# Full attention on one core: the second integer pass over the exponentials moves from VectorE to GpSimd

## The chip, the cores and the metric

The kernel runs on one core of a Trainium2 chip. The core has a matrix engine (TensorE, PE in the profile, with its weight loads as PEld), a vector engine (VectorE, DVE), an activation engine (ScalarE, ACT), a general engine (GpSimd, POOL) and a queue for transfers (SyncE, SP). Each works through its own instructions in a fixed order; semaphores make one wait for another. The metric is the time of one execution on the device in microseconds.

## The reference

Four layers follow each other on x, of shape (1, 2048, 512): a windowed attention A, a full attention B, and both again with the same weights. Each takes the layer-normalized x and adds its result to x. A has 32 heads of 16 and looks at 8 positions, 2 apart. B has 32 query heads of 16 over one shared key and value head; all 2048 positions see all 2048:

```python
q = (x @ wq).reshape(B, S, H, Dh).transpose(0, 2, 1, 3)
k = x @ wk
v = x @ wv
scores = jnp.einsum("bhqd,bkd->bhqk", q, k) * (Dh ** -0.5)
p = _softmax(scores, axis=-1)
o = jnp.einsum("bhqk,bkd->bhqd", p, v)
return o.transpose(0, 2, 1, 3).reshape(B, S, H * Dh) @ wo
```

## The kernel before

The program is two pairs of a stage `Phase` (layer A, and the projections of layer B) and a stage `AttnB` (the full attention). The change lies in `AttnB`.

The scores of layer B are computed transposed, keys on the 128 partitions, 512 queries along the row. A tile of them is 128 keys by 512 queries of one head. Each of 32 segments (4 query chunks, 8 blocks of four heads) has 64 tiles, so a stage has 2048 and the program 4096. Each tile goes through an exponential in one of two ways, and the result is multiplied with the values on TensorE (L1118), with a column of ones beside the values that gives the row sums.

- **By ScalarE.** Two tiles share a PSUM slot `st` (two slots). One exponential instruction (L1099) turns both into bf16 tiles `pt`. Each tile then costs one matmul with the values `VEa`.
- **By VectorE.** A tile sits in a PSUM bank `dv`. The scores are scaled so that adding a constant and storing as 16-bit integers gives the bits of a half-precision number near the exponential: a copy (L1103) writes that into a quarter of a buffer `t`, which holds four tiles. To smooth the approximation, the same integers are taken three times, with offsets of 0, a third and two thirds of 1024 (`J_OFF`), with weights that lie in the values `VEd`. The two shifted versions are made for four tiles at once, by one integer add each (`do_pass`, L1107, a "pass") from `t` into a buffer `i`. Each tile costs three matmuls with the values: one from `t`, two from `i`.

Which tile goes which way, and the order on every engine, is decided while the program is built, by a planner (`Sched` and `Stream`). It plays the engines forward with fixed costs (a copy 600 ns, a pass 133.5 ns a tile and 66, an exponential 426.7 ns a tile and 50, a matmul 216), gives each engine the work that can start first, with small biases, and writes the instructions down in the order of their planned starts. `chain` then holds each engine to that order. `Stream.passes` lists the passes that are ready, `Stream.uses` counts the readers of a buffer (for `t`: its four matmuls and its two passes) until it is free again. There are 14 buffers `pt`, 3 `t` and 5 `i`.

At the end of a segment VectorE copies the sums of the four heads out of PSUM (`X`, L1135). For every second segment the row sums go through transfers (`S`), a reciprocal on VectorE (`R`, L1169) and transfers that spread it (`lb`); GpSimd then scales the rows (`onc`, L1188, 30 times in the program) and adds sums and reciprocals into a check (`chk_b`, L753, 60 times). These are nearly all that GpSimd does in the two stages. After a query chunk comes the output projection (L1205) and its addition to x (L1219).

Of the kernel before, what the change touches and what calls it, by code (L numbers as in the profile page):

```python
# [7 lines left out]
F32 = mybir.dt.float32  # L8
F16 = mybir.dt.float16
I16 = mybir.dt.int16  # L10
AF = mybir.ActivationFunctionType
ALU = mybir.AluOpType
AX = mybir.AxisListType
# [15 lines left out]
NJ = 3  # L29
# [395 lines left out]


MM, SWITCH, DMA = 216.0, 90.0, 620.0
LAT = {"pe": 264.0, "act": 170.0, "dve": 135.0, "pool": 120.0, "sp": 2400.0}
FAR = float("inf")

# [13 lines left out]
class Sched:  # L444
# [68 lines left out]
    def cands(self, e):  # L513
        for op in self.open[e]:
            s = max(op.ready, self.free_at(op.want) if op.want else 0.0)
            s = self.pe_start(op.mode, op.sub, s) if e == "pe" else max(s, self.now[e])
            if s < FAR:
                yield (s + op.prio, s, op.ready, self.issue, (e, op))
        for src in self.sources:
            yield from src.cands(e)  # L520

# [39 lines left out]
class Stream:  # L561
# [5 lines left out]
    def __init__(self, sched, segments, ready, io, res):  # L567
        self.s, self.io = sched, io
        self.segs = segments
        self.tile_ready = ready  # L570
        self.tiles = [(n, kt, g) for n, (_, kts) in enumerate(segments) for kt in kts for g in range(4)]
        self.pos = 0
        self.exps, self.copies, self.passes = [], [], []
# [17 lines left out]
    def cands(self, e):  # L591
        S, B = self.s, self.BIAS
        if e == "pe":
            if self.pos < len(self.tiles):
                tl = self.tiles[self.pos]
                ok = self.tile_ready(self.segs[tl[0]], tl[1])
                if ok < FAR:
                    s = S.pe_start("row", tl[2], max(ok, S.free_at(("slot", "exp"))))
                    if s < FAR:
                        yield (s + B["act2" if self.exps else "act"], s, 0.0, self.fill_slot, None)  # L600
                    s = S.pe_start("row", tl[2], max(ok, S.free_at(("bank", "vec"))))
                    if s < FAR:
                        yield (s + B["vec"], s, 0.0, self.fill_vec, None)
            if self.seg < len(self.segs):
                free = S.free_at(("bank", "o")) if self.bank is None else 0.0
                if free < FAR:
                    for n, (ok, tl, src) in enumerate(self.pvs[self.seg][:24]):
                        s = S.pe_start("col", tl[2], max(ok, free))
                        yield (s + B["pv"] + n * 0.01, s, 0.0, self.pv, n)
        elif e == "act" and self.exps:  # L610
            s = max(S.now["act"], self.exps[0][0], S.free_at(("pt", "exp")))
            if s < FAR:
                yield (s, s, self.exps[0][0], self.exp, None)
        elif e == "dve":
            if self.copies:
                s = max(S.now["dve"], self.copies[0][0])
                if not self.filling:
                    s = max(s, S.free_at(("t", "vec")))
                if s < FAR:
                    late = self.run_of_copies >= 2 and self.passes  # L620
                    yield (s + (B["pass"] if late else B["copy"]), s, 0.0, self.copy, None)
            if self.passes:
                s = max(S.now["dve"], self.passes[0][0], S.free_at(("i", "vec")))
                if s < FAR:
                    yield (s + (0.0 if self.run_of_copies >= 2 else B["pass"]), s, 0.0, self.do_pass, None)

    def fill_slot(self, s, _):
        S, io = self.s, self.io
# [46 lines left out]
    def copy(self, s, _):  # L675
        S, io = self.s, self.io
        _, tl, bank = self.copies.pop(0)
        if not self.filling:
            self.group_buf = S.take(("t", "vec"))
        r, buf = len(self.filling), self.group_buf  # L680
        self.filling.append(tl)
        S.run("dve", s, 600.0)
        done = s + 600 + LAT["dve"]
        S.give(("bank", "vec"), bank, done)
        S.note(s, lambda: io.copy(bank, buf, r))
        self.run_of_copies += 1
        if len(self.filling) == self.GROUP or (self.pos == len(self.tiles) and not self.copies):
            tiles, self.filling = self.filling, []
            self.uses[("t", buf)] = [len(tiles) + NJ - 1, 0.0, ("t", "vec")]
            for j in range(1, NJ):  # L690
                self.passes.append((s + 600, buf, j, tiles))
            for r, tl in enumerate(tiles):
                self.queue(tl, done, ("t", buf, r, 0), 1)

    def do_pass(self, s, _):
        S, io = self.s, self.io
        _, buf, j, tiles = self.passes.pop(0)
        n = len(tiles)
        t = 133.5 * n + 66
        S.run("dve", s, t)  # L700
        out = S.take(("i", "vec"))
        self.uses[("i", out)] = [n, 0.0, ("i", "vec")]
        S.note(s, lambda: io.do_pass(buf, out, j, n))
        self.run_of_copies = 0
        for r, tl in enumerate(tiles):
            self.queue(tl, s + t + LAT["dve"], ("i", out, r, j), j < NJ - 1)
        self.use(("t", buf), s + t)

    def pv(self, s, n):
# [339 lines left out]
class AttnB:  # L1049


    def __init__(self, ctx, tc, QT, KAB, VE, w, x_sb, S, tag, checks, out_view=None):
        self.tc, self.nc, self.w, self.x_sb, self.checks, self.out_view = tc, tc.nc, w, x_sb, checks, out_view
        self.QT, self.KAB, (self.va, self.vd) = QT, KAB, VE
        pool = lambda name, bufs, **kw: ctx.enter_context(tc.tile_pool(name=f"Bf_{name}_{tag}", bufs=bufs, **kw))
        self.slot = [pool(f"st{n}", 1, space=PSUM) for n in range(2)]
        self.bank = [pool(f"bk{n}", 1, space=PSUM) for n in range(4)]
        self.nrm = pool("n", 3)
        self.oncp = pool("c", 2)
        self.drm = pool("d", 2, space=bass.MemoryType.DRAM)  # L1060
# [12 lines left out]
        self.st, self.o, self.dv, self.y, self.tail = {}, {}, {}, {}, {}  # L1073
        self.X, self.onc, self.onb, self.xo = {}, {}, {}, {}
        self.sums, self.ready = {}, {}

    def chain(self, key, inst):
        order_after(self.tc, inst, self.tail.get(key))
# [24 lines left out]
        self.chain("dve", self.nc.vector.tensor_scalar(out=self.t[buf][:, r, :].bitcast(I16), in0=self.dv[bank][:],  # L1103
                                                       scalar1=-U_BIAS, scalar2=U_BIAS, op0=ALU.max, op1=ALU.add))

    def do_pass(self, buf, out, j, n):
        self.chain("dve", self.nc.vector.tensor_scalar(out=self.i[out][:, 0:n, :].bitcast(I16),  # L1107
                                                       in0=self.t[buf][:, 0:n, :].bitcast(I16), scalar1=J_OFF[j],
                                                       scalar2=None, op0=ALU.add))

    def pv(self, bank, at, src, first, last):
        (qc, t, a), kt, g = at
# [216 lines left out]
def kernel(  # L1329
# [13 lines left out]
    nc = tc.nc  # L1343
# [108 lines left out]
```

## Time and profile before

| | |
|---|---|
| timed runs | 1769.97 and 1771.0 us, median 1770.49 |
| profiled execution | span of 1772.6 us from the first to the last instruction |
| first full-attention stage | 208.9 to 883.4 us, 674.5 us |
| second full-attention stage | 1086.4 to 1753.3 us, 666.9 us |
| VectorE copies L1103 | 1332, mean 680 ns |
| VectorE passes L1107 | 668, mean 698 ns |
| ScalarE exponentials L1099 | 1382, mean 1094 ns |
| GpSimd busy, whole span | 206.2 us, 257 instructions |
| mean granted TensorE clock | 0.923 |

The durations of instructions that follow each other on one engine overlap at the ends, so a mean is longer than what one instruction costs in a row of them; the busy time counts each moment once. "Idle before" is the time that the engine stood still ahead of an instruction, with what ended it.

### The profile page before, as it was taken

The page shows a single profiled execution, that of the slowest core. Times are in us where ns is not written, and L with a number is a line of the kernel's source. Part 1 is how long each engine was busy: PE and PEld are TensorE (multiplying, and loading weights), DVE is VectorE, ACT ScalarE, POOL GpSimd, SP SyncE. Part 2 cuts the span into 40 slices and gives each one's busy share as a digit, 9 for nine tenths or more (in the row PEclk, how much of TensorE's full clock was granted, in tenths as well). Part 3 has the DMA queues.
Part 4 walks back from the last instruction along what each step waited for, and adds up shares of the span by engine and source line. Part 5 has one row for each costly group of instructions (what it writes and reads, how often), then busy time and mean ns, then how long its engine had stood idle before and what let it go on. Part 6 is the DMA issues. An engine that isn't in the chain of part 4 may idle for free.

```text
span 1772.6 us, 39835 instructions
## 1 busy us (share of the span) xinstructions
PE 1569.5 (89%) x16214; PEld 539.7 (30%) x16281; DVE 1535.8 (87%) x2565; ACT 1507.3 (85%) x1721; POOL 206.2 (12%) x257
## 2 busy tenths in 40 slices
PE   5776799899999999999977777998999999999996
PEld 3544222222222223222345442222222222222222
DVE  6565499999999999998955646999999999999997
ACT  4654599999999989999856546999999999999994
POOL 4343000000000000000123420000000000000001
PEclk9988799999988999978998878999999899998998
DMA  4000000000000000000000000000000000000000
GB/s 123 3 2 3 0 5 12 17 11 10 12 11 11 11 11 11 11 11 11 11 2 3 2 2 1 11 11 11 11 11 23 11 11 11 23 14 11 11 15 30
DMA packets 40736, 22.96 MB, mean 13 GB/s; under 512 B 28512, under 2 KB 34272, under 8 KB 40544
## 3 DMA queue, kind: packets, MB, share of 16 engines
q1 hardware_dynamic: 39680, 18.50, 4.8%
q8 instruction: 129, 2.11, 0.5%
q10 hardware_dynamic: 864, 1.84, 0.3%
q14 instruction: 63, 0.52, 0.1%
HBM read 13.27 MB, written 2.59 MB: 9 GB/s over the span
## 4 chain that ended last, share of the span: by engine, by line
DVE 59%; PE 26%; ACT 9%; issue 3%; POOL 1%; DMA 0%; DVEq 0%; SPq 0%; ACTq 0%; POOLq 0%
DVE t L1103 32%; DVE i L1107 17%; PE o L1118 9%; PE ps L882 5%; PE st L1084 4%; ACT pt L1099 4%; PE dv L1084 3%; DVE P L951 2%; DVE X L1135 2%; DVE stats L857 2%; ACT P L950 1%; PE pv L910 1%; DVE x_sb L1001 1%; PE dn L980 1%; PE o L961 1%
## 5 line engine op out<-in xcount | busy, mean ns | idle before, releaser
L1099 ACT ACTIVATE pt<-st 128x1024 bf16<-128x1024 f32 x1382 | 1290.7, 1094 | 48.2 <-PE dv L1084 20.4
L1103 DVE TENSOR_SCALAR t<-dv 128x512 int16<-128x512 f32 x1332 | 856.9, 680 | 11.3 <-PE dv L1084 6.2
L1084 PE MATMUL st<-QT,KAB 32*128 32x512 bf16 x2764 | 560.3, 400 | 14.8 <-ACT pt L1099 13.2
L1084 PE MATMUL dv<-QT,KAB 32*128 32x512 bf16 x1332 | 512.9, 397 | 52.2 <-DVE t L1103 38.4
L1118 PE MATMUL o<-pt,VEa 128*32 128x512 bf16 x2764 | 546.3, 412 | 2.7 <-DVE t L1103 1.8
L1118 PE MATMUL o<-i,VEd 128*32 128x512 f16 x2664 | 535.7, 403 | 10.5 <-DVE i L1107 10.1
L1107 DVE TENSOR_SCALAR i<-t 128x2048 int16<-128x2048 int16 x668 | 466.0, 698 | 11.2 <-PE o L1118 0.5
L1084 PEld LDWEIGHTS <-KAB 32*128 32x128 bf16 x4096 | 188.1, 91 | 556.4 <-issue 541.5
L1118 PE MATMUL o<-t,VEd 128*32 128x512 f16 x1332 | 344.7, 407 | 0.2
L1118 PEld LDWEIGHTS <-VEd 128*32 128x32 f16 x3996 | 145.4, 94 | 225.0 <-issue 221.7
L1118 PEld LDWEIGHTS <-VEa 128*32 128x32 bf16 x2764 | 120.2, 94 | 191.9 <-issue 188.9
L753 POOL TENSOR_TENSOR chk_b<-chk_b,S 128x32 f32<-128x32 f32 x30 | 11.0, 367 | 813.6 <-DMA S<-X 684.3
L951 DVE TENSOR_TENSOR P<-P,bandmask 128x1152 bf16<-128x1152 bf16 (+1 forms) x64 | 60.9, 951 | 38.4 <-ACT P L950 37.8
L950 ACT ACTIVATE P<-s 128x1152 bf16<-128x1152 f32 (+1 forms) x64 | 71.8, 1121 | 16.7 <-PE s L945 16.6
L882 PE MATMUL ps<-xnT,w_sb 128*128 128x512 bf16 x233 | 69.2, 427 | 16.8 <-DVE k L898 8.8
L875 PE MATMUL pT<-ident,xn 128*128 128x128 bf16 x256 | 30.6, 263 | 40.4 <-ACT xn L867 23.2
L1188 POOL TENSOR_TENSOR onc<-X,lb 128x512 bf16<-128x512 f32 x30 | 39.8, 1327 | 228.2 <-DMA lb<-rd 214.5
L984 ACT ACTIVATE logs<-dn 128x512 f32<-128x512 f32 x32 | 19.1, 598 | 45.4 <-PE dn L980 45.2
L961 PE MATMUL o<-P,V 64*32 64x72 bf16 (+2 forms) x2176 | 34.9, 209 | 18.9 <-DVE P L951 15.3
L1135 DVE COPY X<-o 128x512 f32<-128x512 f32 x64 | 43.7, 683 | 8.7 <-PE o L1118 8.6
L986 DVE TENSOR_TENSOR onc<-o,rec 128x512 bf16<-128x512 f32 x32 | 22.0, 687 | 33.0 <-ACT rec L985 24.9
L747 POOL TENSOR_TENSOR logs<-logs 128x512 f32<-128x512 f32 x32 | 34.3, 1071 | 130.1 <-ACT rec L985 130.1
(108 smaller groups left out, 871.1 us busy)
## 6 DMA issues: line engine op xcount, KB each, us to landing
lb<-rd SPq DMA_DIRECT2D x240, 32.0 KB, 1.8
S<-X SPq DMA_DIRECT2D x240, 2.0 KB, 1.7
X<-X SPq DMA_DIRECT2D x120, 32.0 KB, 2.0
rd<-R SPq DMA_DIRECT2D x120, 4.0 KB, 1.5
w_sb<-in_A_wqkv_dram ACTq DMA_DIRECT2D x4, 384.0 KB, 5.6
x_bf<-in_A_x_dram SPq DMA_DIRECT2D x3, 512.0 KB, 9.3
out_dram<-xo SPq DMA_DIRECT2D x3, 512.0 KB, 3.0
x_bf<-in_A_x_dram SPq DMA_DIRECT2D x2, 256.0 KB, 5.0
```

Source lines behind the costliest of these rows:

```text
L857: nc.vector.bn_stats(out=stats[:, i, :], in_=src(i))
L882: self.nc.tensor.matmul(ps[:], lhsT=wcols(kt), rhs=xnT[:, kt, :], start=(kt == 0), stop=(kt == 3))
L950: nc.scalar.activation(out=P[:, :, 0:ncol], in_=st[:, :, 0:ncol], func=AF.Exp, scale=DH ** -0.5)
L951: nc.vector.tensor_tensor(out=P[:, :, 0:ncol], in0=P[:, :, 0:ncol], in1=self.w.band[:, 0:ncol].unsqueeze(1).to_broadcast([128, 4, ncol]), ...
L961: nc.tensor.matmul(o[32 * r:32 * r + 32, q0:q0 + w], lhsT=vv[64 * a:64 * a + 64, kb, t, gh, j, :], rhs=P[64 * a:64 * a + 64, g, col:col + ...
L1084: self.chain("pe", self.nc.tensor.matmul(out, lhsT=self.KAB[32 * g:32 * g + 32, a, kt * 128:(kt + 1) * 128], rhs=self.QT[32 * g:32 * g + 3 ...
L1099: self.chain("act", self.nc.scalar.activation(out=self.pt[pt][:, 0:n, :], in_=self.st.pop(key)[:, 0:n, :], func=AF.Exp, scale=E_SCALE))
L1103: self.chain("dve", self.nc.vector.tensor_scalar(out=self.t[buf][:, r, :].bitcast(I16), in0=self.dv[bank][:], scalar1=-U_BIAS, scalar2=U_B ...
L1107: self.chain("dve", self.nc.vector.tensor_scalar(out=self.i[out][:, 0:n, :].bitcast(I16), in0=self.t[buf][:, 0:n, :].bitcast(I16), scalar1 ...
L1118: self.chain("pe", self.nc.tensor.matmul(self.o[bank][32 * g:32 * g + 32, :], lhsT=lhsT, rhs=rhs, start=first, stop=last, tile_position=(0 ...
L1135: self.chain("dve", nc.vector.tensor_copy(out=self.X[qc, t, a][:], in_=self.o.pop(bank)[:]))
L1188: self.chain("pool", nc.gpsimd.tensor_tensor(out=self.onc[qc][:, t, :], in0=self.X[qc, t, 0][:], in1=bufs["lb"][:], op=ALU.mult))
```

## The change

For each group of four tiles the first pass stays on VectorE. The second is done by GpSimd. There it is written as an add of 32-bit integers: two 16-bit values lie in one 32-bit word, and a constant tile `off2` (128 x 4 words, each half holding the offset) is read again and again along the row. The values are not negative and no half overflows into its neighbour, so the sum is the same. A group's row is 1024 words for GpSimd where it was 2048 halves for VectorE.

GpSimd's pass is made to wait for VectorE's pass on the same group (`order_after` with `first_pass`). In the planner a GpSimd pass costs 2.1 ns a word and 120 ns; a new time `port` keeps any pass, on either engine, from being planned before the last planned pass on either has ended. There are seven buffers `i` in place of five. For operations outside the stream (`Op`), the planner's rank now falls by a tenth of the time they have waited.

```diff
@@ Sched.cands
-                yield (s + op.prio, s, op.ready, self.issue, (e, op))
+                yield (s + op.prio - 0.1 * (s - op.ready), s, op.ready, self.issue, (e, op))
@@ Stream.cands
-                s = max(S.now["dve"], self.passes[0][0], S.free_at(("i", "vec")))
+                s = max(S.now["dve"], self.passes[0][0], S.free_at(("i", "vec")), self.port)
                 if s < FAR:
-                    yield (s + (0.0 if self.run_of_copies >= 2 else B["pass"]), s, 0.0, self.do_pass, None)
+                    yield (s + (0.0 if self.run_of_copies >= 2 else B["pass"]), s, 0.0, self.do_pass, "dve")
+        elif e == "pool" and self.pool_passes:
+            s = max(S.now["pool"], self.pool_passes[0][0], S.free_at(("i", "vec")), self.port)
+            if s < FAR:
+                yield (s, s, self.pool_passes[0][0], self.do_pass, "pool")
@@ Stream.copy
-            for j in range(1, NJ):
-                self.passes.append((s + 600, buf, j, tiles))
+            self.passes.append((s + 600, buf, 1, tiles))
@@ Stream.do_pass
-        t = 133.5 * n + 66
-        S.run("dve", s, t)
+        t = 133.5 * n + 66 if e == "dve" else POOL_COL * 256 * n + 120
+        S.run(e, s, t)
+        self.port = s + t
+        if j < NJ - 1:
+            self.pool_passes.append((s + t + LAT["dve"], buf, j + 1, tiles))
...
-            self.queue(tl, s + t + LAT["dve"], ("i", out, r, j), j < NJ - 1)
+            self.queue(tl, s + t + LAT[e], ("i", out, r, j), j < NJ - 1)
@@ AttnB.__init__
-        self.i = [fixed.tile([128, Stream.GROUP, 512], F16, name=f"i{n}") for n in range(5)]
+        self.i = [fixed.tile([128, Stream.GROUP, 512], F16, name=f"i{n}") for n in range(7)]
@@ AttnB
-    def do_pass(self, buf, out, j, n):
-        self.chain("dve", self.nc.vector.tensor_scalar(out=self.i[out][:, 0:n, :].bitcast(I16),
-                                                       in0=self.t[buf][:, 0:n, :].bitcast(I16), scalar1=J_OFF[j],
-                                                       scalar2=None, op0=ALU.add))
+    def do_pass(self, e, buf, out, j, n):
+        if e == "pool":
+            i = self.nc.gpsimd.tensor_tensor(out=self.i[out][:, 0:n, :].bitcast(I32), in0=self.t[buf][:, 0:n, :].bitcast(
+                I32), in1=self.w.off2[:, 0:n].unsqueeze(2).to_broadcast([128, n, 256]), op=ALU.add)
+            order_after(self.tc, i, self.first_pass.pop(buf))
+        else:
+            i = self.nc.vector.tensor_scalar(out=self.i[out][:, 0:n, :].bitcast(I16), in0=self.t[buf][:, 0:n, :].bitcast(
+                I16), scalar1=J_OFF[j], scalar2=None, op0=ALU.add)
+            self.first_pass[buf] = i
+        self.chain(e, i)
@@ kernel
+    w.off2 = cpool.tile([128, 4], I32, name="off2")
+    nc.gpsimd.memset(w.off2[:].bitcast(I16), round(J_OFF[2]))
```

The planner plays out again with these rules, so the order changes on every engine. On VectorE, at the start of the first full-attention stage before (the names carry buffer numbers: `t_3674` is one of the three buffers `t`, `i_3677` one of the buffers `i`; x4 is four instructions alike):

```order
L1103 TENSOR_SCALAR t_3674<-dv 128x512 x4
L1107 TENSOR_SCALAR i_3677<-t_3674 128x2048
L1103 TENSOR_SCALAR t_3675<-dv 128x512 x2
L1107 TENSOR_SCALAR i_3678<-t_3674 128x2048
L1103 TENSOR_SCALAR t_3675<-dv 128x512 x2
L1107 TENSOR_SCALAR i_3679<-t_3675 128x2048
```

The same place on VectorE now, where the lines have moved by some ten:

```order
L1113 TENSOR_SCALAR t_3676<-dv 128x512 x4
L1122 TENSOR_SCALAR i_3679<-t_3676 128x2048
L1113 TENSOR_SCALAR t_3677<-dv 128x512 x4
L1122 TENSOR_SCALAR i_3681<-t_3677 128x2048
L1113 TENSOR_SCALAR t_3678<-dv 128x512 x4
L1122 TENSOR_SCALAR i_3683<-t_3678 128x2048
```

A pass stood behind every two copies and now stands behind every four; each buffer `t` is read once by VectorE where it was read twice. On GpSimd, before, at the first row scaling of the first stage:

```order
L860 TENSOR_TENSOR rstd<-ve,nhalf 128x4
L753 TENSOR_TENSOR chk_b<-chk_b,S_4009 128x32
L753 TENSOR_TENSOR chk_b<-chk_b,R_4422 128x32
L1188 TENSOR_TENSOR onc<-X,lb 128x512
L753 TENSOR_TENSOR chk_b<-chk_b,S_4580 128x32
```

And GpSimd at the same place now (`off_99` is the constant tile):

```order
L1118 TENSOR_TENSOR i_3685<-t_3677,off_99 128x1024
L763 TENSOR_TENSOR chk_b<-chk_b,S_4030 128x32
L1118 TENSOR_TENSOR i_3680<-t_3678,off_99 128x1024
L1118 TENSOR_TENSOR i_3682<-t_3676,off_99 128x1024
L763 TENSOR_TENSOR chk_b<-chk_b,R_4465 128x32
L1118 TENSOR_TENSOR i_3684<-t_3677,off_99 128x1024
L1118 TENSOR_TENSOR i_3679<-t_3678,off_99 128x1024
L1118 TENSOR_TENSOR i_3681<-t_3676,off_99 128x1024
L1118 TENSOR_TENSOR i_3683<-t_3677,off_99 128x1024
L1204 TENSOR_TENSOR onc<-X,lb 128x512
```

The second passes fill GpSimd's order, and the check adds and the row scaling stand among them.

More of the change, by code (lines that the diff above doesn't have):

```diff
@@ L10 @@
 I16 = mybir.dt.int16
+I32 = mybir.dt.int32
 AF = mybir.ActivationFunctionType
@@ L427 @@
 MM, SWITCH, DMA = 216.0, 90.0, 620.0
+POOL_COL = 2.1
 LAT = {"pe": 264.0, "act": 170.0, "dve": 135.0, "pool": 120.0, "sp": 2400.0}
@@ L572, in __init__ @@
         self.pos = 0
-        self.exps, self.copies, self.passes = [], [], []
+        self.exps, self.copies, self.passes, self.pool_passes = [], [], [], []
+        self.port = 0.0
         self.res = res
@@ L689, in copy, with do_pass @@
             self.uses[("t", buf)] = [len(tiles) + NJ - 1, 0.0, ("t", "vec")]
-            for j in range(1, NJ):
-                self.passes.append((s + 600, buf, j, tiles))
+            self.passes.append((s + 600, buf, 1, tiles))
             for r, tl in enumerate(tiles):
                 self.queue(tl, done, ("t", buf, r, 0), 1)
-    def do_pass(self, s, _):
+    def do_pass(self, s, e):
         S, io = self.s, self.io
-        _, buf, j, tiles = self.passes.pop(0)
+        _, buf, j, tiles = (self.passes if e == "dve" else self.pool_passes).pop(0)
         n = len(tiles)
-        t = 133.5 * n + 66
-        S.run("dve", s, t)
+        t = 133.5 * n + 66 if e == "dve" else POOL_COL * 256 * n + 120
[3 more added lines that the diff above has]
+            self.pool_passes.append((s + t + LAT["dve"], buf, j + 1, tiles))
         out = S.take(("i", "vec"))
         self.uses[("i", out)] = [n, 0.0, ("i", "vec")]
-        S.note(s, lambda: io.do_pass(buf, out, j, n))
-        self.run_of_copies = 0
+        S.note(s, lambda: io.do_pass(e, buf, out, j, n))
+        if e == "dve":
+            self.run_of_copies = 0
         for r, tl in enumerate(tiles):
-            self.queue(tl, s + t + LAT["dve"], ("i", out, r, j), j < NJ - 1)
+            self.queue(tl, s + t + LAT[e], ("i", out, r, j), j < NJ - 1)
         self.use(("t", buf), s + t)
@@ L1074, in __init__ @@
         self.X, self.onc, self.onb, self.xo = {}, {}, {}, {}
-        self.sums, self.ready = {}, {}
+        self.sums, self.ready, self.first_pass = {}, {}, {}
     def chain(self, key, inst):
```

## The prediction

> **What bounds the kernel now.** I read the page's busy times first, then the span cut into its stages, then the groups of instructions, and last single stretches in order of time. On the page three engines look equally full:
>
> ```profile
> PE 1569.5 (89%) x16214; PEld 539.7 (30%) x16281; DVE 1535.8 (87%) x2565; ACT 1507.3 (85%) x1721; POOL 206.2 (12%) x257
> ```
>
> The change touches only the two full-attention stages. The windows cut at the first and last VectorE work of each (columns: window, length, then busy time and count of PE, PEld, DVE, ACT, POOL, and the granted TensorE clock) show them:
>
> ```profile
> 208.90:883.40 674.50, 637.87 (x5466) 178.78 (x5472) 656.45 (x1087) 647.98 (x693) 35.43 (x49) 0.93 0.05 11
> 1086.40:1753.30 666.90, 624.15 (x5463) 178.99 (x5469) 651.01 (x1060) 643.09 (x692) 33.20 (x47) 0.95 0.06 13
> 260.00:300.00 40.00, 38.26 (x346) 10.60 (x345) 39.66 (x66) 40.00 (x44) 1.96 (x4) 1.00 0.05 10
> 1680.00:1700.00 20.00, 20.00 (x198) 6.20 (x195) 19.79 (x34) 20.00 (x24) 0.75 (x2) 1.00 0.09 19
> ```
>
> The stages are 674.5 + 666.9 = 1341.4 us of the span, and GpSimd is 5% busy there. VectorE and ScalarE are at 97% and 96%: they share the score tiles, and the planner has balanced them. Where nothing disturbs, ScalarE is busy without a gap and does 44 instructions in 40.00 us, 0.909 us each. The groups say what those instructions are:
>
> ```profile
> L1099 ACT ACTIVATE pt<-st 128x1024 bf16<-128x1024 f32 x1382 | 1290.7, 1094 | 48.2 <-PE dv L1084 20.4
> L1103 DVE TENSOR_SCALAR t<-dv 128x512 int16<-128x512 f32 x1332 | 856.9, 680 | 11.3 <-PE dv L1084 6.2
> L1107 DVE TENSOR_SCALAR i<-t 128x2048 int16<-128x2048 int16 x668 | 466.0, 698 | 11.2 <-PE o L1118 0.5
> ```
>
> Spans overlap at their ends, so what an instruction costs is the spacing of starts, which a VectorE stretch in order of time gives (start, length, instruction):
>
> ```profile
> 434.13 1.28 DVE L1103 TENSOR_SCALAR t<-dv 128x512 int16<-128x512 f32 x2
> 435.32 0.17 DVE L858 BATCH_NORM_AGGREGATE mv<-stats 128x2 f32<-128x6 f32 x1
> 435.44 0.69 DVE L1107 TENSOR_SCALAR i<-t 128x2048 int16<-128x2048 int16 x1
> 436.05 1.28 DVE L1103 TENSOR_SCALAR t<-dv 128x512 int16<-128x512 f32 x2
> 437.25 1.72 DVE L1107 TENSOR_SCALAR i<-t 128x2048 int16<-128x2048 int16 x1
> 438.89 1.28 DVE L1103 TENSOR_SCALAR t<-dv 128x512 int16<-128x512 f32 x2
> ```
>
> A copy is 0.60 us (437.25 - 436.05 is two), a pass 0.61 (436.05 - 435.44). Per group of four tiles VectorE pays 4 x 0.60 + 2 x 0.61 = 3.62 us, 0.905 a tile; ScalarE pays 0.909 / 2 = 0.455 a tile. Per stage ScalarE needs 691 x 0.909 = 628 us of the mean 670.7, so 42.6 us are lost to the start, the end and disturbances.
>
> **The port.** The pass at 437.25 lasted 1.72 us. GpSimd was at work beside it:
>
> ```profile
> 437.15 1.27 POOL L1188 TENSOR_TENSOR onc<-X,lb 128x512 bf16<-128x512 f32 x1 [6.67 <-DMA lb<-rd]
> 651.69 1.26 POOL L1188 TENSOR_TENSOR onc<-X,lb 128x512 bf16<-128x512 f32 x1 [7.89 <-DMA lb<-rd]
> 651.16 1.28 DVE L1103 TENSOR_SCALAR t<-dv 128x512 int16<-128x512 f32 x2
> ```
>
> GpSimd ended at 438.42, and the pass 0.55 us later, at 438.97: it stood still until GpSimd was done. The copies beside the operation at 651.69 kept their 1.28 us for two. So a pass and a GpSimd operation exclude each other here, a copy out of PSUM and a GpSimd operation do not.
>
> **The change, part by part.** By the order of instructions, VectorE copies go from 1332 to 1428 (+96), its passes from 668 to 358 (-310), ScalarE's exponentials from 1382 to 1334 (-48), and GpSimd gets 358 passes, two of them half size. TensorE's matmuls on these tiles go from 2 x 2764 + 4 x 1332 = 10856 to 2 x 2668 + 4 x 1428 = 11048.
>
> - **ScalarE**: 48 x 0.909 = 43.6 us less. If ScalarE is the last to finish, this is the gain.
> - **VectorE**: 96 x 0.60 - 310 x 0.61 = -131 us. It comes off a bound engine, but only 43.6 us of it can show, since ScalarE is next. VectorE is then some 12% idle and no longer sets the end.
> - **GpSimd's pass**: no row shows an integer add. The nearest are float operations with two different inputs, beside a small one that gives the fixed part (count: shortest/median/longest ns):
>
> ```profile
> L753 POOL TENSOR_TENSOR chk_b<-chk_b,S x30: 249/251/806, 259.6 to 1718.4; 128x32 f32<-128x32 f32 x30
> L1188 POOL TENSOR_TENSOR onc<-X,lb x30: 1262/1270/1771, 272.1 to 1730.7; 128x512 bf16<-128x512 f32 x30
> L747 POOL TENSOR_TENSOR logs<-logs x32: 1032/1039/1519, 42.2 to 1038.6; 128x512 f32<-128x512 f32 x32
> ```
>
> From 32 to 512 elements is 251 to 1270 ns, 2.12 ns an element; 1024 packed pairs are 251 + 992 x 2.12 = 2.36 us. The low bound is the square at L747, 1032 ns: 1.63 ns an element, 1.86 us. The high bound takes the longest row, 1771 ns: 3.17 ns, 3.39 us. I take 2.36, since that row also reads two tensors and is a median of 30. A recorded end can be checked: the pass held at 437.25 ended 0.55 us after GpSimd's recorded end, and a free pass lasts 0.69, so the port came free at most 0.14 us before that end and not after it. The Trainium skill (Perfetto Trace Analysis, GPSIMD Engine Instruction) calls the span of a GpSimd instruction in a profile unreliable. By that rule 2.36 could be off by more than the 0.24 us of cover found below, and then the sum would lose 36 us for each 0.1 us beyond it; by the held pass it is right within 0.14, and the sum stands.
>
> - **The wait**: a GpSimd pass waits for VectorE's pass on the same group. Behind it on GpSimd stand the next groups' passes, the 60 check adds and the 30 row scalings; who waits for it are the matmuls on its tile, and VectorE's next pass through the port. The signal's price is in these rows:
>
> ```profile
> 264.51 0.34 DVE L1169 RECIPROCAL R<-S 128x32 f32<-128x32 f32 x1
> 264.94 0.25 POOL L753 TENSOR_TENSOR chk_b<-chk_b,R 128x32 f32<-128x32 f32 x1 [4.55 <-DVE R L1169]
> ```
>
> VectorE ends at 264.85, GpSimd starts at 264.94: about 0.1 us. So the port's round is 0.55 (a released pass) + 0.1 + 2.36 = 3.01 us a group. VectorE has 4 copies and a pass between two passes, 3.01 us as well, so at full speed the next pass arrives as GpSimd ends. ScalarE's pace is slower: 1334 x 0.909 over 357 groups is 3.40 us a group. The port is covered, with 0.39 us a group to spare. The other GpSimd work takes it for 15 x (1.27 + 2 x 0.25) = 27 us a stage, 0.15 a group; 0.24 is left. If that cover is gone (a pass of over 2.6 us), each further 0.1 us costs 36 us.
>
> - **TensorE**: 192 matmuls more, at nothing, hidden under ScalarE: needed are 11048 in about 1300 us, 170 per 20 us, and the window at 1680 above shows 198 with ScalarE full.
> - **The ends**: the last second pass of a stage, on two tiles, goes from about 0.4 us on VectorE to 251 + 480 x 2.12 = 1.27 us on GpSimd; +1 us twice. Seven i buffers for five, the aged priorities and one more small memset at the start move nothing that ends late: nothing.
>
> Sum on the profiled execution: 1772.6 - 43.6 + 2 = 1731.0. The timed runs' median, 1770.49, lies 2.1 us below the profiled span, so the forecast is 1770.5 - 41.6 = **1729 us**, its own range 1712 to 1745 (a gain from 25 to 58 us: the 42.6 us a stage of losses grow or shrink by a fifth).
>
> **The rivals.**
>
> - **Held passes halve TensorE's clock (slower).** This is in the trace already. After the operation at 437.15 held a pass:
>
> ```profile
> 436.60:440.00 3.40, 2.04 (x12) 0.41 (x11) 3.40 (x5) 3.24 (x4) 1.27 (x1) 0.97 0.00 0
> 440.00:443.40 3.40, 3.40 (x17) 0.73 (x20) 3.27 (x7) 2.06 (x3) 0.00 (x0) 0.50 0.00 0
> 443.40:446.80 3.40, 3.40 (x29) 0.51 (x21) 3.37 (x7) 2.85 (x3) 0.00 (x0) 0.52 0.04 7
> ```
>
> TensorE fell to 12 matmuls in 3.4 us, and the clock was then 0.50 for the next two windows; ScalarE lost 10.2 - 8.15 = 2.05 us. If half of the 90 places where GpSimd's other operations stand between passes end like this, that is 45 x 2.05 = 92 us: 1729 + 92 = 1821. It undoes the gain from 20 events on. For it: the clock's mean is only 0.93 and 0.95 in the stages now. Against: the order places a pass behind a GpSimd pass where the planner thinks the port free. The Trainium skill (TensorE: Matmul & The Clock Gate, Part 1) has the clock fall to half after an idle window of about 3.4 us; the rows agree, with 12 matmuls enough to count as idle. Chance 0.10.
> - **The port becomes the bound (slower).** The Trainium skill warns that moving work between VectorE and GpSimd might not help, since they share a port (Perfetto Trace Analysis, Optimizing Scalar/DVE Operations). From the rows: a stage of 178.5 groups takes 178.5 x (0.65 + p) + 27 us for a GpSimd pass of p. It reaches the present 670.7 at p = 2.96 us, and at 2.72 if the 42.6 us of other losses stay. At the high bound, 3.39, it is 748 us even without them, 155 us more for both: 1925. For it: no row prices the integer form. Against: two of three rows lie far below. Chance 0.10.
> - **TensorE is the bound.** It is 94% busy in the stages. At the present pace, 11048 / 10856 x 1341.4 = 1365 us, 24 us more: 1794. For it: the busy share. Against: the 198. Chance 0.14.
> - **Nothing follows from the freed time.** ScalarE starves as often as it is relieved, since a GpSimd pass comes out 2.4 us later and TensorE takes its work in a fixed order: 1770. Chance 0.06.
> - **The losses go too.** Two balanced engines disturb each other; if VectorE's slack takes away half of the 42.6 us a stage, 43 us more are gained: 1686. Chance 0.10.
>
> **How the numbers follow.** The forecast keeps 0.50. A measurement of this kernel tells 2% from no change, 35 us: below 1735 is faster, above 1806 slower. Faster: 0.10 and four fifths of 0.50, together 0.50. Slower: the 0.20 of the two slow cases, less 0.03 for a clock's case that stays small: 0.17. Same: the rest, 0.33. The range, 1685 to 1800, holds the forecast, the bound TensorE, the unused time and the upper case; it leaves out the two slow cases.
>
> **What would show it.** Right: GpSimd's pass near 2.36 us and 0.1 us behind VectorE's; VectorE's passes still near 0.69 us in the mean; ScalarE at 96% or more of both stages, the stages at 649 us each. Wrong: VectorE passes of 1 us and more in the mean (the port); the clock below 0.9 in the stages (the clock); TensorE waiting on the GpSimd tiles with ScalarE under 94%; a GpSimd pass above 2.8 us.

## The result, and the profile after

The changed kernel takes 1708.55 us (two runs, 1708.33 and 1708.78) against 1770.49 before: a ratio of 0.9651, with a 95% interval of 0.9623 to 0.9679, or 62 us less. The forecast was 1729, its range 1685 to 1800. The direction was right and the gain half as large again as forecast. The profiled execution's span fell from 1772.6 to 1707.0 us.

Page of the changed kernel, busy times, and then its groups of instructions:

```profile
PE 1534.6 (90%) x16473; PEld 524.4 (31%) x16473; DVE 1424.3 (83%) x2351; ACT 1451.7 (85%) x1673; POOL 874.4 (51%) x616
...
L1109 ACT ACTIVATE pt<-st 128x1024 bf16<-128x1024 f32 x1334 | 1235.4, 1126 | 35.3 <-PE st L1094 15.7
L1118 POOL TENSOR_TENSOR i<-t,off 128x1024 int32<-128x1024 int32 x358 | 676.6, 1890 | 540.7 <-DVE i L1122 284.5
L1113 DVE TENSOR_SCALAR t<-dv 128x512 int16<-128x512 f32 x1428 | 891.3, 679 | 51.3 <-PE o L1134 36.0
```

GpSimd's pass takes 1.89 us in the mean, where 2.36 had been taken. The counts are the ones read from the order.

The two stages, cut as before (window, length, busy time and count of PE, PEld, DVE, ACT, POOL, granted clock):

```profile
207.50:844.90 637.40, 611.80 (x5573) 172.62 (x5565) 595.36 (x952) 617.20 (x668) 367.40 (x226) 0.98 0.05 12
1050.30:1688.10 637.80, 613.28 (x5573) 171.99 (x5565) 594.34 (x953) 617.90 (x668) 367.37 (x226) 0.98 0.06 14
```

They last 637.4 + 637.8 = 1275.2 us where they lasted 1341.4, 66.2 us less; the span fell by 65.6, so all of it is in the stages. ScalarE is busy for 97% of them (96% before), VectorE for 93% (97% before), and the granted clock is 0.98, not 0.93 and 0.95.

The chain of waits that ended last, by engine, of the kernel before:

```profile
DVE 59%; PE 26%; ACT 9%; issue 3%; POOL 1%; DMA 0%; DVEq 0%; SPq 0%; ACTq 0%; POOLq 0%
```

and of the changed kernel:

```profile
PE 40%; DVE 27%; ACT 25%; issue 7%; POOL 1%; DVEq 0%; ACTq 0%; POOLq 0%
```

The prediction did not read this view. Before, the chain ran through VectorE for 59% of the span and through ScalarE for 9%: the two engines were equally busy, but VectorE was the one waited for. Now they have 27% and 25%.

VectorE and GpSimd of the changed kernel in order of time (start, length, instruction):

```profile
307.08 0.69 DVE L1122 TENSOR_SCALAR i<-t 128x2048 int16<-128x2048 int16 x1
307.69 2.47 DVE L1113 TENSOR_SCALAR t<-dv 128x512 int16<-128x512 f32 x4
310.20 0.69 DVE L1122 TENSOR_SCALAR i<-t 128x2048 int16<-128x2048 int16 x1
...
314.52 2.47 DVE L1113 TENSOR_SCALAR t<-dv 128x512 int16<-128x512 f32 x4
317.03 1.71 DVE L1122 TENSOR_SCALAR i<-t 128x2048 int16<-128x2048 int16 x1
```

```profile
307.94 1.89 POOL L1118 TENSOR_TENSOR i<-t,off 128x1024 int32<-128x1024 int32 x1 [1.91 <-PE o L1134]
311.06 1.89 POOL L1118 TENSOR_TENSOR i<-t,off 128x1024 int32<-128x1024 int32 x1 [1.23 <-DVE i L1122]
315.07 1.89 POOL L1118 TENSOR_TENSOR i<-t,off 128x1024 int32<-128x1024 int32 x1 [2.12 <-PE dv L1094]
316.92 1.27 POOL L1204 TENSOR_TENSOR onc<-X,lb 128x512 bf16<-128x512 f32 x1
```

VectorE's pass ends at 307.77 and GpSimd's starts at 307.94, runs beside the four copies and has ended at 309.83, before the next pass at 310.20. From 317.03 on the main kind of collision that is left can be seen: a row scaling stands right behind a GpSimd pass, runs from 316.92 to 318.19, and holds the pass of 317.03 until 318.74, again 0.55 us after GpSimd's recorded end. By a count in the trace, 28 of the 358 passes last over 0.8 us, 25 of them held by a row scaling.

For what follows, one count in the traces is needed: the stages' sum less the number of exponentials times 0.909 us is what ScalarE **loses**. Before it is 1342.1 - 1382 x 0.909 = 85.9 us for both stages, after 1276.4 - 1334 x 0.909 = 63.8 (sums here are cut at the first copy and the last sum copied out, up to 1.2 us longer than the windows).

### The profile page after: what moved, and what is told of

Its sections match the earlier page's. It is cut to its first block, busy times and chain, and to the rows that moved or that the text cites. A ratio compares the mean times of both kernels' runs of the same rounds, so it can differ in the third digit from the quotient of the medians.

```text
span 1707.0 us, 40879 instructions
## 1 busy us (share of the span) xinstructions
PE 1534.6 (90%) x16473; PEld 524.4 (31%) x16473; DVE 1424.3 (83%) x2351; ACT 1451.7 (85%) x1673; POOL 874.4 (51%) x616
## 4 chain that ended last, share of the span: by engine, by line
PE 40%; DVE 27%; ACT 25%; issue 7%; POOL 1%; DVEq 0%; ACTq 0%; POOLq 0%
ACT pt L1109 20%; DVE t L1113 16%; PE o L1134 14%; PE st L1094 9%; PE dv L1094 6%; PE ps L892 5%; DVE P L961 2%; DVE stats L867 2%; ACT P L960 2%; DVE i L1122 2%; PE y L1221 1%; DVE x_sb L1011 1%; PE pv L920 1%; PE dn L990 1%; PE o L971 1%
## 5 line engine op out<-in xcount | busy, mean ns | idle before, releaser
L1109 ACT ACTIVATE pt<-st 128x1024 bf16<-128x1024 f32 x1334 | 1235.4, 1126 | 35.3 <-PE st L1094 15.7
L1118 POOL TENSOR_TENSOR i<-t,off 128x1024 int32<-128x1024 int32 x358 | 676.6, 1890 | 540.7 <-DVE i L1122 284.5
L1113 DVE TENSOR_SCALAR t<-dv 128x512 int16<-128x512 f32 x1428 | 891.3, 679 | 51.3 <-PE o L1134 36.0
L1134 PE MATMUL o<-i,VEd 128*32 128x512 f16 x2856 | 564.1, 392 | 0.0
L1094 PE MATMUL dv<-QT,KAB 32*128 32x512 bf16 x1428 | 526.9, 388 | 37.3 <-DVE t L1113 28.1
L1094 PE MATMUL st<-QT,KAB 32*128 32x512 bf16 x2668 | 526.8, 388 | 14.2 <-ACT pt L1109 11.7
L1134 PE MATMUL o<-pt,VEa 128*32 128x512 bf16 x2668 | 530.2, 393 | 0.7 <-DVE t L1113 0.5
L1134 PE MATMUL o<-t,VEd 128*32 128x512 f16 x1428 | 369.5, 392 | 0.0
L1122 DVE TENSOR_SCALAR i<-t 128x2048 int16<-128x2048 int16 x358 | 263.7, 736 | 10.4
L1134 PEld LDWEIGHTS <-VEd 128*32 128x32 f16 x4284 | 138.4, 94 | 267.6 <-issue 265.4
L1134 PEld LDWEIGHTS <-VEa 128*32 128x32 bf16 x2668 | 118.1, 94 | 157.1 <-issue 152.7
L757 POOL TENSOR_TENSOR logs<-logs 128x512 f32<-128x512 f32 x32 | 35.3, 1104 | 126.0 <-ACT rec L995 126.0
L870 POOL TENSOR_TENSOR rstd<-ve,nhalf 128x4 f32<-128x4 f32 x16 | 16.3, 1016 | 82.7 <-DVE ve L869 79.8
```

The source lines that it names most:

```text
L757: self.nc.gpsimd.tensor_tensor(out=logs, in0=logs, in1=logs, op=ALU.mult)
L1094: self.chain("pe", self.nc.tensor.matmul(out, lhsT=self.KAB[32 * g:32 * g + 32, a, kt * 128:(kt + 1) * 128], rhs=self.QT[32 * g:32 * g + 3 ...
L1109: self.chain("act", self.nc.scalar.activation(out=self.pt[pt][:, 0:n, :], in_=self.st.pop(key)[:, 0:n, :], func=AF.Exp, scale=E_SCALE))
L1118: i = self.nc.gpsimd.tensor_tensor(out=self.i[out][:, 0:n, :].bitcast(I32), in0=self.t[buf][:, 0:n, :].bitcast(I32), in1=self.w.off2[:, 0: ...
L1122: i = self.nc.vector.tensor_scalar(out=self.i[out][:, 0:n, :].bitcast(I16), in0=self.t[buf][:, 0:n, :].bitcast(I16), scalar1=J_OFF[j], sca ...
L1134: self.chain("pe", self.nc.tensor.matmul(self.o[bank][32 * g:32 * g + 32, :], lhsT=lhsT, rhs=rhs, start=first, stop=last, tile_position=(0 ...
```

## The experiments

The open question: why 62 us and not 42? The prediction's theory is that ScalarE sets the end, and that only the 48 exponentials taken off it count. The rival is that VectorE set the end before, that its relief is worth something by itself, and that it is still among the engines that set the end.

**The old share of tiles, the new way of passing.** The planner may give VectorE no more tiles than it had; all else is as changed.

```diff
-                    if s < FAR:
+                    if s < FAR and (self.n_vec <= 0.3252 * self.pos or self.pos > len(self.tiles) - 24):
```

> The changed kernel, with the planner held to the old share of tiles: 1380 ScalarE exponentials and 1336 VectorE copies, while GpSimd still does the second passes. If ScalarE sets the pace, 46 more exponentials at 0.909 us cost 42 us: about 1750. If the gain comes from the relief of VectorE or from the higher clock alone, whatever the share, it stays at 1708 to 1720.

Measured: 1743.89 us, ratio 0.983 (0.9786 to 0.9874), about 30 us less than before. ScalarE has 1380 exponentials, two fewer than before. Its stages and its chain:

```profile
208.02:863.57 655.55, 597.49 (x5476) 186.30 (x5478) 575.88 (x896) 636.18 (x691) 347.43 (x214) 0.98 0.05 11
1071.91:1723.73 651.82, 595.02 (x5476) 186.55 (x5478) 576.44 (x895) 635.56 (x691) 347.25 (x214) 0.98 0.06 14
...
ACT 60%; PE 18%; issue 10%; DVE 8%; POOL 2%; DMA 1%; SPq 0%; POOLq 0%; ACTq 0%
```

This is the state that the prediction drew for the changed kernel: ScalarE sets the end (60% of the chain), VectorE is 12% idle. It is reached with no tile moved, and it is worth 34 us of the stages by itself, as ScalarE's loss falls from 85.9 to 53.0. What the relief does shows on TensorE, which works in a fixed order for both engines. Its matmuls into the banks `dv`, in the kernel before and in this one (busy time, mean ns, and the idle time before them with what ended it):

```profile
L1084 PE MATMUL dv<-QT,KAB 32*128 32x512 bf16 x1332 | 512.9, 397 | 52.2 <-DVE t L1103 38.4
L1094 PE MATMUL dv<-QT,KAB 32*128 32x512 bf16 x1336 | 517.3, 389 | 4.3 <-DVE VEd L1037 3.4 <-DVE t L1113 0.9
```

TensorE stood still there for VectorE's copies for 38.4 us and does for 0.9 in this kernel. The clock of the stages is 0.98 as well; how much of the 30 us came through the clock was not separated.

The time is far above the rival's, for which the relief was nearly everything, but the forecast of the whole change had no term for these 30 us either: both terms are there. The step from here to the changed kernel, 46 exponentials, is worth 0.983 - 0.9651 = 1.8%, 32 us, or 0.69 us for each and not 0.909.

**More work for VectorE.** A part of each group's second copy is done a second time: 256 columns, estimated at 0.33 us, 358 times, 118 us in all.

```diff
+        if r == 1:
+            self.chain("dve", self.nc.vector.tensor_scalar(out=self.t[buf][:, r, 0:256].bitcast(I16),
+                                                           in0=self.dv[bank][:, 0:256], scalar1=-U_BIAS,
+                                                           scalar2=U_BIAS, op0=ALU.max, op1=ALU.add))
```

> The changed kernel, with one more VectorE copy of 256 columns (about 0.33 us, the same values written again) in each of 357 groups, 118 us of VectorE work that the planner doesn't know of. If VectorE has slack and ScalarE sets the pace, 0 to 25 us show: 1708 to 1734. If VectorE still sets the pace, all of it: about 1826.

Measured: 1865.07 us, ratio 1.053 (1.0461 to 1.0599), some 155 us more than the changed kernel. The work added is more than the 118 us of the estimate, as a stretch of VectorE shows:

```profile
308.28 0.69 DVE L1126 TENSOR_SCALAR i<-t 128x2048 int16<-128x2048 int16 x1
308.89 1.28 DVE L1113 TENSOR_SCALAR t<-dv 128x512 int16<-128x512 f32 x2
310.20 0.42 DVE L1116 TENSOR_SCALAR t<-dv 128x256 int16<-128x256 f32 x1
310.55 1.28 DVE L1113 TENSOR_SCALAR t<-dv 128x512 int16<-128x512 f32 x2
311.86 0.69 DVE L1126 TENSOR_SCALAR i<-t 128x2048 int16<-128x2048 int16 x1
```

A round of VectorE takes 311.86 - 308.28 = 3.58 us here and 3.12 in the changed kernel: 0.46 us more in each of 358 groups, or 165 us. Its chain, and ScalarE's exponentials:

```profile
DVE 53%; PE 31%; issue 8%; ACT 6%; POOL 1%; DVEq 0%; ACTq 0%; POOLq 0%
...
L1109 ACT ACTIVATE pt<-st 128x1024 bf16<-128x1024 f32 x1334 | 1275.3, 1035 | 140.0 <-PE st L1094 85.2
```

ScalarE waits 140.0 us ahead of its exponentials, where it waited 35.3. So the slack that the prediction saw on VectorE could not be used for this work: of 165 us, 155 show, and VectorE's idle time in the stages is 1421.2 - 1330.2 = 91.0 us, where the changed kernel has 85.5. (The mean clock is 0.917 here and 0.951 in the changed kernel, and the extra copy holds its PSUM bank longer; what either adds was not separated.)

**Without the wait.** GpSimd's pass is not made to wait for VectorE's; the order on each engine stays.

```diff
-            order_after(self.tc, i, self.first_pass.pop(buf))
```

> The changed kernel without GpSimd's wait for VectorE's pass on the same group; the order on each engine is the same. If GpSimd now gets the port first, each VectorE pass is held for up to 1.89 us; the group then takes VectorE 2.40 + 1.89 + 0.55 = 4.84 us against 3.57 now, and the time goes to about 2150. If VectorE gets it first in nearly all groups, since its pass follows its last copy with no signal between engines, the time stays within 10 us of 1708.

Measured: 1773.49 us, ratio 1.0001 (0.997 to 1.0032). The whole gain is gone. Two places of its trace, VectorE first and GpSimd after:

```profile
285.71 2.07 DVE L1121 TENSOR_SCALAR i<-t 128x2048 int16<-128x2048 int16 x1
287.71 2.47 DVE L1113 TENSOR_SCALAR t<-dv 128x512 int16<-128x512 f32 x4
290.10 2.07 DVE L1121 TENSOR_SCALAR i<-t 128x2048 int16<-128x2048 int16 x1
...
304.27 0.69 DVE L1121 TENSOR_SCALAR i<-t 128x2048 int16<-128x2048 int16 x1
```

```profile
285.34 1.89 POOL L1118 TENSOR_TENSOR i<-t,off 128x1024 int32<-128x1024 int32 x1 [1.59 <-DVE t L1113]
289.73 1.89 POOL L1118 TENSOR_TENSOR i<-t,off 128x1024 int32<-128x1024 int32 x1 [2.49 <-DVE t L1113]
...
304.40 2.31 POOL L1118 TENSOR_TENSOR i<-t,off 128x1024 int32<-128x1024 int32 x1 [3.58 <-DVE t L1113]
```

Both passes become ready when the copies are done. Where VectorE comes first (304.27), it takes its 0.69 us and GpSimd's pass is stretched to 2.31. Where GpSimd comes first (285.34), it takes its 1.89 us and VectorE's pass is held to 2.07, ending 0.55 us after GpSimd's; a group then takes 290.10 - 285.71 = 4.39 us on VectorE and not 310.20 - 307.08 = 3.12. The Trainium skill (SBUF — State Buffer, SBUF: two separate sides) says that the shared port goes whole to the instruction that starts first and that the other blocks; both rows agree, one for each winner. By a count in the trace VectorE comes first in most groups: 299 of GpSimd's 358 passes last over 2.1 us (2 in the changed kernel). Only 66 of VectorE's 358 passes last over 0.8 us (28 in the changed kernel), 46 of them held by a GpSimd pass, and the passes' time above 0.69 us adds up to 63.6 us (17.5). So holds in one group of eight go with the loss of the whole gain. They make up 46 of the 62 us or so; where the rest comes from was not separated. The stages' clock is 0.95 and ScalarE's loss 124 us.

**GpSimd's pass half as long again.** Half of each pass is done a second time: 3.01 us for both parts.

```diff
+            for m in (n, n // 2):
+                i = self.nc.gpsimd.tensor_tensor(out=self.i[out][:, 0:m, :].bitcast(I32), in0=self.t[buf][:, 0:m, :].bitcast(
+                    I32), in1=self.w.off2[:, 0:m].unsqueeze(2).to_broadcast([128, m, 256]), op=ALU.add)
...
```

> The changed kernel, with half of GpSimd's pass done once more right behind it, which makes it about 1.89 + 1.0 = 2.9 us without the planner knowing. If the port then binds: a round of 0.55 + 0.1 + 2.95 and 0.15 of other GpSimd work is 3.75 us against 3.57 now, so the stages take at least 357 x 0.18 = 64 us more: 1772 or above. If the wait is covered by ScalarE's pace with room: 1708 to 1725.

Measured: 1824.99 us, ratio 1.0313 (1.0272 to 1.0354).

```profile
305.75 1.27 DVE L1125 TENSOR_SCALAR i<-t 128x2048 int16<-128x2048 int16 x1
306.95 2.47 DVE L1113 TENSOR_SCALAR t<-dv 128x512 int16<-128x512 f32 x4
309.45 1.27 DVE L1125 TENSOR_SCALAR i<-t 128x2048 int16<-128x2048 int16 x1
```

```profile
303.47 3.01 POOL L1119 TENSOR_TENSOR i<-t,off 128x1024 int32<-128x1024 int32 x2 [1.18 <-DVE i L1125]
307.17 3.01 POOL L1119 TENSOR_TENSOR i<-t,off 128x1024 int32<-128x1024 int32 x2
```

Most passes now wait for GpSimd (261 of 358 last over 0.8 us), and the round is 309.45 - 305.75 = 3.70 us; the prediction's port formula gives 0.65 + 3.01 = 3.66. Its stage, 178.5 x 3.66 + 27 = 680 us, stands against 691 and 698 measured. So the port does become the bound, where the prediction put it; the integer add is simply too short for that.

**The rest of the change alone.** The kernel before with seven buffers `i` and the aged priorities.

```diff
-                yield (s + op.prio, s, op.ready, self.issue, (e, op))
+                yield (s + op.prio - 0.1 * (s - op.ready), s, op.ready, self.issue, (e, op))
...
-        self.i = [fixed.tile([128, Stream.GROUP, 512], F16, name=f"i{n}") for n in range(5)]
+        self.i = [fixed.tile([128, Stream.GROUP, 512], F16, name=f"i{n}") for n in range(7)]
```

> The kernel before with only the two edits that are not the pass: seven buffers i and the aged priorities. Both passes stay on VectorE, and the share of tiles is the old one. If they carry none of the gain: 1770, within 8 us. If the aged priorities (evacuations and additions earlier or later on VectorE) explain a part of what isn't the tile share: down to 1750.

Measured: 1775.37 us, ratio 1.0031 (1.0004 to 1.0058): none of the gain.

**Without the planner's port time.** `self.port = s + t` is taken out of the changed kernel; the wait stays.

> The changed kernel with a planner that lets a VectorE pass be planned while GpSimd's is under way (no port time); GpSimd's wait for VectorE's pass on the same group stays. If a VectorE pass that meets GpSimd's stands still for up to 1.89 us and upsets TensorE's order, this loses most of the gain: 1740 to 1770. If the wait alone keeps the two apart, since four copies last longer than GpSimd's pass: 1708 to 1720.

Measured: 1710.81 us, ratio 0.9672 (0.9638 to 0.9705), as the changed kernel. The planner made another order of it, with 12 exponentials more and 24 copies fewer. The passes' time above 0.69 us is 14.8 us (17.5 in the changed kernel), so the wait alone keeps the passes apart, and the planner's knowledge of the port brings nothing that can be measured. The 12 exponentials, 10.9 us at 0.909, cost nothing that can be measured either: ScalarE loses 49.1 us in place of 63.8.

**A dearer pass in the planner.** Behind four copies a VectorE pass costs 310.20 - 307.69 - 4 x 0.60 + 0.61 = 0.72 us, 0.11 more than the planner has, since it now always reads the copy just ahead of it. The planner is told so:

```diff
-        t = 133.5 * n + 66 if e == "dve" else POOL_COL * 256 * n + 120
+        t = 133.5 * n + 176 if e == "dve" else POOL_COL * 256 * n + 120
```

> The changed kernel, with VectorE's pass priced in the planner at 710 ns in place of 600, near the 0.72 us that it takes now that it follows the copy whose output it reads. If the planner's too low price makes VectorE late against the order: 10 to 25 us less, down to 1685 to 1700. If ScalarE alone sets the pace: 1708, within 8 us.

Measured: 1713.57 us, ratio 0.968 (0.9633 to 0.9727): no gain.

**Held passes, before the change.** In the kernel before, each row scaling on GpSimd is cut into four of 128 columns, so that none can hold a pass for long.

```diff
+            for c in range(4):
+                cs = slice(128 * c, 128 * c + 128)
+                self.chain("pool", nc.gpsimd.tensor_tensor(out=self.onc[qc][:, t, cs], in0=self.X[qc, t, 0][:, cs],
+                                                           in1=bufs["lb"][:, cs], op=ALU.mult))
```

> The kernel before, with each row scaling on GpSimd (1.27 us) cut into four of 128 columns (about 0.45 us each), so that a VectorE pass is held 0.45 us at most and not 1.27. If single long holds are what starves TensorE and halves its clock, the stages' clock rises from 0.93 and 0.95 to about 0.97, with up to 15 us less: about 1756. If the clock falls for another reason (VectorE without slack), the time stays at 1770 and the clock with it.

Measured: 1764.68 us, ratio 0.9933 (0.9906 to 0.9961), a gain of some 10 us, where up to 15 were expected; the clock of the stages is 0.94 and 0.97. Held passes cost time before the change.

**What the pass on GpSimd costs where it is.** Four kernels on one chip, of which the first is the changed kernel again. In the second GpSimd's pass is left out, and the matmuls that read its result read that of VectorE's pass; the second shifted version is thus not computed.

```diff
-            i = self.nc.gpsimd.tensor_tensor(out=self.i[out][:, 0:n, :].bitcast(I32), in0=self.t[buf][:, 0:n, :].bitcast(
-                I32), in1=self.w.off2[:, 0:n].unsqueeze(2).to_broadcast([128, n, 256]), op=ALU.add)
-            order_after(self.tc, i, self.first_pass.pop(buf))
+            self.alias[out] = self.alias[self.first_pass.pop(buf)]
+            return
```

> The changed kernel unchanged, as the base for the other three on the same chip. All theories: about 1709 us, a ratio of 0.965 to the kernel before.

> The changed kernel with GpSimd's pass left out: the matmuls that read its result read that of VectorE's pass instead, so the second shifted version is not computed and this only measures what the pass costs where it is. Matmuls, copies, exponentials and their order stay. Theory that the kernel now ends by VectorE and ScalarE together and the pass on GpSimd is fully hidden: 1703 to 1709 us, nothing but a few holds gone. Rival, that what ScalarE still loses (64 us over both stages) is due to the pass, by holding VectorE's pass or coming late to TensorE: 1665 to 1690 us.

Measured: the changed kernel 1710.35 us, ratio 0.9662 (0.9629 to 0.9696); without GpSimd's pass 1697.67, ratio 0.9583 (0.955 to 0.9617). Leaving the pass out altogether saves 12.7 us, a little more than the theory that it is hidden, and far less than its rival. The third and fourth kernel tell what those 12.7 us are: the changed kernel with the row scalings in four pieces, and the same without the planner's port time.

> The changed kernel with each of GpSimd's 30 row scalings (1.27 us) cut into four pieces of 128 columns, so that a VectorE pass that meets one is held for a quarter of the time. Before the change the same cut was worth 0.7%. Theory that held passes still cost time now, each by what follows it on TensorE: 5 to 12 us less than the changed kernel, 1697 to 1704. Rival, that with the passes kept apart by the wait these 30 places matter little: 1707 to 1711.

> The changed kernel without the planner's port time (alone within the noise of the changed kernel) and with the row scalings in four pieces. If the losses at held passes count: 1697 to 1704 us, the fastest version here. If they do not: 1707 to 1713, as without the port time alone.

Measured: with the pieces 1701.04 us (four runs from 1699.35 to 1703.18, against 1708.28 to 1711.99 for the changed kernel beside it), ratio to before 0.9603 (0.957 to 0.9637). It is the fastest version here that computes everything, about 9 us below the changed kernel. With the pieces and without the port time: 1707.86, ratio 0.9647 (0.9613 to 0.9681), which can't be told from the changed kernel. This order, too, has 12 exponentials more and 24 copies fewer. The passes' time above 0.69 us falls only from 14.8 to 8.2 us in it; whether that is all of why the pieces gain less stays open.

VectorE's passes in the changed kernel, in the one with pieces, and in the one without GpSimd's pass:

```profile
L1122 DVE TENSOR_SCALAR i<-t 128x2048 int16<-128x2048 int16 x358 | 263.7, 736 | 10.4
```

```profile
L1122 DVE TENSOR_SCALAR i<-t 128x2048 int16<-128x2048 int16 x358 | 254.1, 710 | 10.4
```

```profile
L1121 DVE TENSOR_SCALAR i<-t 128x2048 int16<-128x2048 int16 x358 | 251.4, 702 | 10.4
```

The passes lose 9.6 and 12.3 us of holds, and the time falls by 9.3 and 12.7: in these two, a microsecond that a pass is held is about a microsecond of the run. (It is no fixed price: in the kernel before, the pieces took 4.0 us off the passes and some 10 us off the run.) Leaving the pass out gains only some 3 us more than the pieces do. So most of what GpSimd's pass still costs is by delaying row scalings into VectorE's next pass, and the pass itself, 676.6 us of work, costs within some 3 us of nothing.

## Why the prediction was right, and where it was not

- **GpSimd's pass** was sized too dear: 1.89 us where 2.36 was taken, at the low bound of 1.86. The row that fits is the square at L747, not the one with two inputs. It follows VectorE's pass by 0.17 us and not 0.1. The port's round is then 0.55 + 0.17 + 1.89 = 2.61 us, half a microsecond below VectorE's own round of 3.12, so the port was covered by more than the prediction thought. The rival of the port as the bound was refuted by that size; at 3.01 us it is what happens.
- **VectorE's relief** was put at -131 us and is 656.45 + 651.01 - 595.36 - 594.34 = 117.8 us of busy time. About half of the difference is holds: the passes' time above 0.69 us is 17.5 us now against 10.1 before.
- **"It comes off a bound engine, but only 43.6 us of it can show"** is the step that failed, and with it the 42.6 us a stage of losses that were carried over unchanged. Those losses were in good part ScalarE waiting for VectorE by way of TensorE; the falls of the clock are part of them. With no tile moved, the relief alone is worth 30 us. The 46 exponentials that are then moved bring 32 us and not 46 x 0.909 = 41.8: they load VectorE again, and ScalarE's loss rises from 53.0 to 63.8. In sum the losses fell by 22.1 us: 43.6 + 22.1 is the 65.7 of the stages. The forecast's own range for the losses, a fifth up or down (17 us, 1712 to 1745), was a little too narrow. The rival in which half of them go gave 1686; a quarter went.
- **"VectorE is then some 12% idle and no longer sets the end"**: it is 7% idle, and 165 us more work for it cost 155 us. By the prediction's own terms it would have been 9% idle, (1307.5 - 131) us in 1341.4 - 43.6; the 12% hold for the old length of the stages. The idle time that is left was not filled by that work; 36.0 us of the 51.3 ahead of its copies ended with TensorE's matmuls at L1134, which read the buffers `t`. The chain of waits of before, 59% on VectorE and 9% on ScalarE, said that its relief would count for itself.
- **TensorE's 192 matmuls** showed no cost that could be seen: at the old pace the stages would have lasted 1365 us, and they last 1275. How much TensorE, at 40% of the chain, takes of them now was not separated.
- **The held passes and the clock**: the clock in the stages rose to 0.98. The holds came all the same, 25 behind row scalings, where the rival let 20 undo the gain; but the pieces, which shorten them, gained 9 us and not 25 x 2.05 = 51. The mechanism is real where the passes themselves collide: without the wait they are held and the clock is 0.95. What prevented that is the wait, not the planner's port time on which the prediction's counterargument rested.
- **The rest, priced at nothing**, was nothing or less (+0.3%, with an interval that just leaves out zero). The +1 us at each stage's end is too small to be seen beside the rest.

What stays open: ScalarE still loses 49 us with no GpSimd pass at all. In four kernels the loss goes down with the time that the clock stood at half in the stages (by a count in the traces 150 us before, 55 after, 34 with the pieces, 27 without the pass, for losses of 86, 64, 52 and 49). It does not in all: without the wait, 140 us at half the clock stand beside a loss of 124. No run tells which of the two follows the other.

## What to carry to other kernels

Where two engines share the work and both are 97% busy, the busy shares don't say which one is waited for; the chain of waits did here, and relieving that engine also takes away part of what the other seemed to lose by itself. A share of the chain is no price, though: with 27% of it in the changed kernel, VectorE still paid for nearly all the work that was added to it. Work moved from VectorE to GpSimd can be nearly free if the two are made to take turns at the port, GpSimd beside VectorE's copies out of PSUM; the same work without that wait gained nothing here. After such a move, look for what now stands right behind GpSimd's new work: cutting the 1.27 us row scalings into four pieces brought another 0.5%.

## What was not expected of the hardware

The lengths of GpSimd's pass in the changed kernel (shortest, median and longest in ns, and the two sizes):

```profile
L1118 POOL TENSOR_TENSOR i<-t,off x358: 1039/1892/2339, 211.0 to 1686.5; 128x1024 int32<-128x1024 int32 x178, 128x512 int32<-128x512 int32 x1
```

- The 32-bit integer add with a second input that repeats costs (1892 - 1039) / 512 = 1.67 ns a word, where the float operations with two full inputs cost 2.12 an element; 354 of the 356 full-sized passes lie between 1891 and 1895 ns. (The two sizes in the line are counted in one stage.)
- A recorded length of GpSimd's contains its wait for the port: 2.31 us beside a VectorE pass, 1.89 without one.
- A VectorE pass that reads the copy just ahead of it costs 0.72 us, and 0.61 when other copies lie between. The change removed the cheap ones: of the two passes of a group, the second had come two copies later. The prediction had 0.61 for every pass, and so 3.01 us for a round that takes 3.12.
